# Reordering the opening of a fused attention and two-MLP kernel, and moving batch 1's preparation one step

## The chip, the cores and the metric

One core of one Trainium2 chip runs the whole kernel. The metric is the device time of one execution in microseconds, the median of three runs. The profile is one execution on the same core.

## The reference

All arrays are float32. There are 8 batches of 576 rows and 512 columns (8 heads of 64).

```python
kv = einsum('bhsd,bhse->bhde', k, v)            # 64 x 64 for each head
out = einsum('bhsd,bhde->bhse', q, kv)
out = out / sqrt(mean(out**2, -1) + 1e-6) * g_norm
x = out as (batch, 576, 512)
u = x + real(fft(fft(x, axis=1), axis=2))       # mixing by a 2D transform
un = (u - mean(u)) / sqrt(var(u) + 1e-6)        # over the 512 columns
x2 = u + max(un @ w_ch1, 0) @ w_ch2             # 512 -> 2048 -> 512
u2 = x2 + (x2.T @ U @ V).T                      # rank 32, over the rows
result = u2 + max(u2 @ w2_ch1, 0) @ w2_ch2
```

## The kernel before

**Stages.** The 4608 rows form 9 blocks of 512. A batch is prepared first: the products of keys and values (`kvbd`), the outputs `o` (`t_o`), their norm (`t_norm`), the folds of rows and columns that halve the transform (`t_fold_s`, `t_fold_e`), the high and low parts of the folded columns (`t_fold_h`, `t_fold_l`), the transform over the rows (`t_s1`), and that over the columns (`t_s2`). The first MLP then goes through each block in 16 steps, one for each 128 of the 2048 hidden columns: `emit_l1(n)` makes hidden chunk n by 12 matrix products, `emit_l2(n - 1)` adds the chunk before to four accumulators. The second MLP follows, its last part in groups that don't matter here.

**Order.** The order of instructions is written by hand; each engine takes its own in that order. The opening (`tile_fused_kernel` from line 1220 on) prepares batch 0 whole and normalises and transposes block 0 (`f_stats`, `f_rs`, `f_norm`, `f_tr`), before step 0 starts. `keep_warm(n)` puts n products of the identity, two instructions each, between TensorE's real ones. Batch j + 1 is prepared in the steps of block j: `batch_tasks(b)` gives a list of tasks for each step, and `place` appends them to `side[n]`, which runs at the end of step n. `fill[n]` runs ahead of `emit_l2(n - 1)`. In a step the order is: split of the second weight, `emit_l1(n)`, `w_mags` for the weights that this step converts, `split_w1(n + 2)`, `fill[n]`, `emit_l2(n - 1)`, `side[n]`.

**Weights.** Weights arrive as 64-bit words (the arrays viewed as integers, 512 KB each) and are converted to float32 on the chip: `w_load` (SyncE's queue), `w_mags` (two ScalarE instructions, lines 113 and 114), `conv_a` (VectorE, lines 122 and 123), `conv_b` (VectorE line 128, then the addition of line 130 on VectorE or, for the second of a pair, on GpSimd). Weight 2i is chunk i of the first matrix, 2i + 1 of the second. In step k of block 0 `w_conv` converts weights 6 + 2k and 7 + 2k. `split_w1` takes the high part on ScalarE (line 198) and the low part on GpSimd or VectorE (line 199). There are two `raw` buffers and two `more_raw`; converting a weight frees its buffer, and `w_next` issues the next load.

**Buffers that tie the stages.** `side_bank` gives PSUM banks: in the opening four accumulator banks and two side banks in turn, from step 0 on the two side banks alone. The tables of the transform (`load_table`) land in buffers and are rounded by ScalarE (`round_table`, line 297). The single row 288 has its own tile `e288`, whose high half ScalarE and low half VectorE writes (lines 448 and 461); a product of line 473 reads it. Key and value rows of batches 1 to 4 are loaded early by `kv_load_early`, into buffers of weights that come later.

Batch 1 is one step later than the other batches (`SH = 1`), in these lines:

```python
d = SH if b == 1 else 0
t[c + d][0:0] = [lambda k=k: t_o(b, k) for k in ks]
t[c + d + 4 + p].append(lambda c=c, p=p: t_fold_l(b, c, p))
if d and p:
    fill[9] = lambda: [t_s1(b, 1, e) for e in range(2)]
else:
    t[7 + d + p] += [lambda p=p, e=e: t_s1(b, p, e) for e in range(2)]
```

Of the kernel before, what the change touches and what calls it, by code (L numbers as in the profile page):

```python
# [23 lines left out]
C = 128  # L24
# [21 lines left out]
def kernel(ctx: ExitStack, tc: tile.TileContext, qT, kvm, gn, w1a, w2a, w1b, w2b,  # L46
# [280 lines left out]

    kvt = {}
# [213 lines left out]
    def load_first():  # L542
        kv = at.tile([128, 2, KC, DM], F32, tag="slot_a", name="kv0")
        q = whole(at, [128, 4, NQ], F32, "q0", "slot_c")
        for half in range(2):
            c = slice(256 * half, 256 * half + 256)
            for a in range(2):
                nc.sync.dma_start(out=kv[:, a, :, c], in_=kvm[0][:, a, :, c])
        nc.sync.dma_start(out=q, in_=qT[0])
# [9 lines left out]
    def batch_tasks(b):  # L559

        t = [[] for _ in range(14)]
        d = SH if b == 1 else 0
# [11 lines left out]
        for p in range(2):  # L574
            if d and p:
                fill[9] = lambda: [t_s1(b, 1, e) for e in range(2)]
            else:
                t[7 + d + p] += [lambda p=p, e=e: t_s1(b, p, e) for e in range(2)]
# [49 lines left out]
    def f_new():  # L628
        for w in (6, 2, 1, "b"):
            first[w] = whole(pa, [128, 5, 1 if w == "b" else w], F32, f"first{w}", f"lnf{w}")  # L630
        nc.vector.memset(first[2], 1.0)
# [10 lines left out]
    def f_norm(i):  # L642
# [6 lines left out]
        if i < 3:  # L649
# [570 lines left out]
    with tc.manual_schedule():  # L1220
# [6 lines left out]
        load_table(0)  # L1227
        kv_load_early(1, 6)
        load_table(1)
        load_table(2)  # L1230
        kv_load_early(2, 11)
        for k in range(4):
            w_load(k)
# [7 lines left out]
        keep_warm(15)  # L1241
        t_kv(0, 0)
        t_kv(0, 1)
        for k in range(5):
            t_o(0, k)
        keep_warm(60)
# [6 lines left out]
        round_table(0, 0)  # L1253
# [3 lines left out]
        t_fold_h(0, 1, 0)  # L1257
        t_fold_l(0, 0, 0)
# [3 lines left out]
        t_fold_l(0, 1, 0)  # L1262
        t_fold_l(0, 2, 0)
# [3 lines left out]
        round_table(1, 0)  # L1267
        for c in range(2):
            t_fold_s(0, c, 1)
            t_fold_e(0, c, 1)  # L1270
            if c:
                t_s1_hi(0, 0, 0)
            t_fold_h(0, c, 1)
            if c:
                t_s1_hi(0, 0, 1)
                t_fold_l(0, 0, 1)
            else:
                round_table(2, 0)
        t_fold_s(0, 2, 1)
        t_fold_e(0, 2, 1)  # L1280
        t_fold_h(0, 2, 1)
        t_fold_l(0, 1, 1)
        t_fold_l(0, 2, 1)
        for e in range(2):
            t_s1_lo(0, 0, e)
            round_table(2, 1 + e)
        for e in range(2):
            t_s1(0, 1, e)
        t_s2(0, 2)
# [3 lines left out]
        w_mags(0, 1, 2, 3)  # L1293
# [14 lines left out]
        for i in range(3):  # L1308
            f_norm(i)
        a0 = conv_a(raws.pop(0), w_new(0), pws.pop(0))  # L1310
        for i in (3, 4):
            f_norm(i)
        conv_b(*a0)
        w_next((0,))
# [9 lines left out]
        w_conv(3, 4)  # L1324
# [213 lines left out]
```

## Time and profile before

| | us |
|---|---|
| median of 3 runs (1761.09 to 1761.47) | 1761.33 |
| the profiled execution | 1760.34 |
| its span, first to last instruction | 1758.4 |
| TensorE busy in the span | 1737.7 |
| VectorE busy | 1180.2 |
| ScalarE busy | 832.0 |
| GpSimd busy | 463.8 |

PE is TensorE, DVE VectorE, ACT ScalarE, POOL GpSimd, and L473 is line 473 of the kernel. A float32 product is two instructions, one of the rounded type `fp32r` is one. TensorE's busy time counts the `warm` products too, and its matrix products overlap at their ends, so that the starts in a timeline tell more than the lengths. A row of a timeline gives start, length, engine, line, operation, output and inputs, shape, count, and in brackets the idle time before it and what ended that.

### The profile page before, as it was taken

To read this page: it belongs to the slowest core of one execution; us is meant where nothing else is said; L and a number is where in the kernel's file an instruction comes from. 1 tells how busy PE (TensorE), PEld (TensorE's weight loads), DVE (VectorE), ACT (ScalarE), POOL (GpSimd) and SP (SyncE) were. 2 spreads that over 40 slices of the span, in tenths; PEclk is the share of its full clock that TensorE was granted. 3 is DMA by queue.
4 is the path that set the end of the run, shared out by engine and by line. 5 is a ranking of instruction groups with operands and counts; after the bars stand their busy time and mean duration, and the time that the engine had idled before them with its cause. 6 is when DMAs were issued, how large, how long until landed. Compare 5 with 4: busy or idle time off the path is not lost.

```text
span 1758.4 us, 23273 instructions
## 1 busy us (share of the span) xinstructions
PE 1737.7 (99%) x8246; PEld 1428.3 (81%) x8246; DVE 1180.2 (67%) x1913; ACT 832.0 (47%) x1594; POOL 463.8 (26%) x362
## 2 busy tenths in 40 slices
PE   9999999999999999999999999999999999999999
PEld 9767788888888888888888788878888888888877
DVE  5878777778677686756676667348735963694285
ACT  5674344544334343443555465455345534552253
POOL 2346454554645445442322222000000000000000
PEclk9999999999999999999999999999999999999999
DMA  8755124150613415004378854757776776777675
GB/s 321 239 183 202 49 99 140 37 196 29 222 52 139 156 66 205 25 37 118 111 271 296 315 205 161 243 170 254 244 233 197 242 256 181 224 220 237 190 218 189
DMA packets 130276, 315.25 MB, mean 179 GB/s; under 512 B 20696, under 2 KB 23528, under 8 KB 128368
## 3 DMA queue, kind: packets, MB, share of 16 engines
q1 hardware_dynamic: 130160, 313.77, 53.7%
q8 instruction: 65, 1.06, 0.2%
q14 instruction: 51, 0.42, 0.1%
HBM read 238.83 MB, written 74.88 MB: 178 GB/s over the span
## 4 chain that ended last, share of the span: by engine, by line
PE 93%; DMA 3%; DVE 2%; ACT 1%; issue 1%; SPq 0%; POOL 0%; ACTq 0%; DVEq 0%; POOLq 0%
PE y L1118 10%; PE yy L1198 10%; PE h L223 8%; PE h L225 8%; PE h L224 8%; PE acc L252 7%; PE acc L254 7%; PE acc L253 7%; PE z L1198 5%; PE zz L1118 5%; PE w L1198 3%; PE z L1118 3%; PE o L383 2%; PE pt L814 1%; PE acc L244 1%; PE u L839 1%
## 5 line engine op out<-in xcount | busy, mean ns | idle before, releaser
L199 POOL TENSOR_TENSOR w1l<-w,w1h 128x512 fp32r<-128x512 f32 x147 | 199.2, 1355 | 404.1 <-ACT w1h L198 391.7
L223 PE MATMUL h<-xl,w1h 128*128 128x512 f32 x576 | 232.0, 403 | 2.7 <-DVE xl L668 2.7
L225 PE MATMUL h<-xh,w1l 128*128 128x512 f32 x576 | 226.0, 392 | 0.0
L224 PE MATMUL h<-xh,w1h 128*128 128x512 f32 x576 | 225.5, 392 | 0.0
L252 PE MATMUL acc<-w2h,gl 128*128 128x512 f32 x524 | 205.9, 393 | 0.1
L254 PE MATMUL acc<-w2h,gh 128*128 128x512 f32 x524 | 204.1, 389 | 0.0
L253 PE MATMUL acc<-w2l,gh 128*128 128x512 f32 x524 | 204.0, 389 | 0.0
L232 ACT ACTIVATE gh<-h 128x512 fp32r<-128x512 f32 x147 | 87.7, 596 | 228.4 <-PE h L225 227.9
L1118 PE MATMUL y<-xv,v 128*128 128x512 f32 x768 | 191.8, 394 | 2.7 <-ACT g L1055 2.7
L1055 ACT ACTIVATE g<-y 128x512 f32<-128x512 f32 x128 | 76.7, 599 | 211.5 <-PE y L1118 211.5
L1118 PEld LDWEIGHTS y<-xv,v 128*128 128x128 f32 x768 | 143.6, 187 | 38.4 <-ACT g L1055 4.5
L233 DVE SCALAR_TENSOR_TENSOR gl<-h,gh 128x512 fp32r<-128x512 f32 x147 | 100.7, 685 | 88.3 <-ACT gh L232 88.0
L209 DVE TENSOR_TENSOR w2l<-w,w2h 128x512 fp32r<-128x512 f32 x147 | 136.1, 926 | 26.8 <-ACT w2h L208 26.4
L223 PEld LDWEIGHTS h<-xl,w1h 128*128 128x128 f32 x576 | 109.1, 189 | 24.9 <-issue 4.1
L225 PEld LDWEIGHTS h<-xh,w1l 128*128 128x128 f32 x576 | 108.7, 189 | 24.4 <-POOL w1l L199 0.6
L224 PEld LDWEIGHTS h<-xh,w1h 128*128 128x128 f32 x576 | 109.1, 189 | 22.3 <-issue 1.7
L252 PEld LDWEIGHTS acc<-w2h,gl 128*128 128x128 f32 x524 | 98.3, 188 | 21.8 <-DVE gl L233 2.1
L254 PEld LDWEIGHTS acc<-w2h,gh 128*128 128x128 f32 x524 | 98.4, 188 | 20.6
L253 PEld LDWEIGHTS acc<-w2l,gh 128*128 128x128 f32 x524 | 98.4, 188 | 19.8
L198 ACT ACTIVATE w1h<-w 128x512 fp32r<-128x512 f32 x160 | 99.9, 624 | 25.8 <-DVE w L130 21.5
L208 ACT ACTIVATE w2h<-w 128x512 fp32r<-128x512 f32 x147 | 91.8, 625 | 34.8 <-PE acc L254 31.2
L1049 DVE TENSOR_TENSOR g<-zz,g 128x512 f32<-128x512 f32 x64 | 44.2, 691 | 93.1 <-ACT g L1055 80.1
(237 smaller groups left out, 3675.0 us busy)
## 6 DMA issues: line engine op xcount, KB each, us to landing
v<-wv_d SPq DMA_DIRECT2D x224, 512.0 KB, 3.8
wv_d<-vo SPq DMA_DIRECT2D x112, 256.0 KB, 2.8
kve<-in_kvm SPq DMA_DIRECT2D x40, 256.0 KB, 6.8
q<-in_qT SPq DMA_DIRECT2D x8, 1220.0 KB, 10.5
x_d<-x2o SPq DMA_DIRECT2D x36, 256.0 KB, 2.1
x2f<-x_d SPq DMA_DIRECT2D x36, 256.0 KB, 5.1
outT<-o SPq DMA_DIRECT2D x36, 256.0 KB, 2.4
u_d<-x SPq DMA_DIRECT2D x32, 256.0 KB, 2.6
```

Of the source, the lines that this page charges most:

```text
L198: nc.scalar.activation(out=ah, in_=a, func=AF.Copy)
L199: (nc.vector if n in on_dve else nc.gpsimd).tensor_tensor(out=al, in0=a, in1=f32(ah), op=ALU.subtract)
L209: nc.vector.tensor_tensor(out=cl, in0=c, in1=f32(ch), op=ALU.subtract)
L223: nc.tensor.matmul(out=h, lhsT=ah[:, kc, :], rhs=xl[:, kc, :], start=(kc == 0), stop=False)
L224: nc.tensor.matmul(out=h, lhsT=ah[:, kc, :], rhs=xh[:, kc, :], start=False, stop=False)
L225: nc.tensor.matmul(out=h, lhsT=al[:, kc, :], rhs=xh[:, kc, :], start=False, stop=(kc == 3))
L233: nc.vector.scalar_tensor_tensor(out=gl, in0=h, scalar=0.0, in1=f32(gh), op0=ALU.max, op1=ALU.subtract)
L252: nc.tensor.matmul(out=a, lhsT=gl[:, tt], rhs=ch, start=s, stop=False)
L253: nc.tensor.matmul(out=a, lhsT=gh[:, tt], rhs=cl, start=False, stop=False)
L254: nc.tensor.matmul(out=a, lhsT=gh[:, tt], rhs=ch, start=False, stop=e)
L1118: nc.tensor.matmul(out=dst, lhsT=w[:, c], rhs=r[:, k], start=p in (0, 1, 3) and k + n == 0, stop=k == 1 and n == 2, skip_group_check=True)
L1198: nc.tensor.matmul(out=dst[mp], lhsT=w[:, c], rhs=r, start=p in (0, 1, 6, 3) and i + n == 0, stop=i == 7 and n == 2, skip_group_check=True)
```

## The change

The change touches the opening and steps 0 to 9.

- **Batch 0's loads.** Keys and values come in five row tiles instead of four quarters by columns; q in two pieces. The tables are loaded ahead of batch 1's keys and values, and weight 0 ahead of them too; weights 1 to 3 ahead of batch 2's.
- **Batch 0's products** of keys and values are accumulated tile by tile in one bank (`t_kv_first`), with one copy of each half into `kvbd`. Of the warm products 8 and 52 are left of 15 and 60.
- **Pauses.** The tables are rounded at other places, weight 0's magnitudes are taken and weight 0 is converted ahead of the column transform instead of between the norms of block 0. The folds of the second kind start earlier. The norm of the third part (`f_norm(2)`) moves from ScalarE to VectorE.
- **Small tiles.** `first[1]` and `first["b"]` share one tile.
- **Batch 1.** Outputs, norms and folds start in step 0 (`d = 0`); its row transform stays in step 8 and `fill[9]` (`d1 = SH`).
- **Weights 3 to 7.** `w_conv(4, 3)` takes weight 4 first, so that its addition is VectorE's and weight 3's GpSimd's; the conversion of weight 5 and the magnitudes of 6 and 7 go behind batch 1's tasks in step 0's list.

```diff
@@ -324,6 +324,18 @@
             nc.scalar.activation(out=kvbd[64:128, pairs, 64:128], in_=pv[64:128, :, 64:128], func=AF.Copy)
         else:
             nc.vector.tensor_copy(out=kvbd[64:128, pairs, 64:128], in_=pv[64:128, :, 64:128])
+
+    def t_kv_first():
+        kv = st[0]["kv"]
+        ps = side_bank("kv0")
+        for t in range(KC):
+            for j in range(4):
+                cols = slice(128 * j, 128 * j + 128)
+                nc.tensor.matmul(out=ps[:, cols], lhsT=kv[:, 0, t, cols], rhs=kv[:, 1, t, cols],
+                                 start=(t + j == 0), stop=(t == KC - 1), skip_group_check=True)
+        pv = ps.rearrange("p (j e) -> p j e", j=4)
+        nc.scalar.activation(out=kvbd[0:64, :, 0:64], in_=pv[0:64, :, 0:64], func=AF.Copy)
+        nc.vector.tensor_copy(out=kvbd[64:128, :, 64:128], in_=pv[64:128, :, 64:128])
 
     kvt = {}
 
@@ -542,11 +554,10 @@
     def load_first():
         kv = at.tile([128, 2, KC, DM], F32, tag="slot_a", name="kv0")
         q = whole(at, [128, 4, NQ], F32, "q0", "slot_c")
-        for half in range(2):
-            c = slice(256 * half, 256 * half + 256)
-            for a in range(2):
-                nc.sync.dma_start(out=kv[:, a, :, c], in_=kvm[0][:, a, :, c])
-        nc.sync.dma_start(out=q, in_=qT[0])
+        for t in range(KC):
+            nc.sync.dma_start(out=kv[:, :, t], in_=kvm[0][:, :, t])
+        for c in (slice(0, 2 * C), slice(2 * C, NQ)):
+            nc.sync.dma_start(out=q[:, :, c], in_=qT[0][:, :, c])
         nc.sync.dma_start(out=gnb, in_=gn)
         st[0] = {"kv": kv, "q": q}
 
@@ -559,7 +570,7 @@
     def batch_tasks(b):
 
         t = [[] for _ in range(14)]
-        d = SH if b == 1 else 0
+        d, d1 = 0, SH if b == 1 else 0
         for c in range(3):
             ks = range(2 * c, min(2 * c + 2, 5))
             t[c + d][0:0] = [lambda k=k: t_o(b, k) for k in ks]
@@ -572,10 +583,10 @@
                 t[c + d + 4 + p].append(lambda c=c, p=p: t_fold_l(b, c, p))
             t[c + 9].append(lambda c=c: t_s2(b, c))
         for p in range(2):
-            if d and p:
+            if d1 and p:
                 fill[9] = lambda: [t_s1(b, 1, e) for e in range(2)]
             else:
-                t[7 + d + p] += [lambda p=p, e=e: t_s1(b, p, e) for e in range(2)]
+                t[7 + d1 + p] += [lambda p=p, e=e: t_s1(b, p, e) for e in range(2)]
         if b + 1 < B:
             if b + 1 in EARLY:
                 t[11].insert(0, lambda: kv_back(b + 1))
@@ -626,8 +637,10 @@
         nc.vector.bn_aggr(out=first[2][:m, i], in_=first[6][:m, i])
 
     def f_new():
-        for w in (6, 2, 1, "b"):
-            first[w] = whole(pa, [128, 5, 1 if w == "b" else w], F32, f"first{w}", f"lnf{w}")
+        for w in (6, 2):
+            first[w] = whole(pa, [128, 5, w], F32, f"first{w}", f"lnf{w}")
+        rb = whole(pa, [128, 2, 5, 1], F32, "firstr", "lnfr")
+        first[1], first["b"] = rb[:, 0], rb[:, 1]
         nc.vector.memset(first[2], 1.0)
 
     def f_rs(a, b):
@@ -646,7 +659,7 @@
             z = whole(at, [C, 3, ND], F32, "un_z", "de", 2)
             un[0].insert(0, z.rearrange("p a b -> p (a b)")[:, 0:DM])
         x = st[0]["x"][:m, g, c]
-        if i < 3:
+        if i < 2:
             nc.scalar.activation(out=un[0][i][:m], in_=x, func=AF.Identity, bias=first["b"][:m, i],
                                  scale=first[1][:m, i])
         else:
@@ -1224,13 +1237,13 @@
         nc.vector.memset(f32(e288), 0.0)
         nc.scalar.activation(out=e288, in_=f32(e288), func=AF.Copy)
         load_first()
-        load_table(0)
+        for k in range(3):
+            load_table(k)
+        w_load(0)
         kv_load_early(1, 6)
-        load_table(1)
-        load_table(2)
+        for k in (1, 2, 3):
+            w_load(k)
         kv_load_early(2, 11)
-        for k in range(4):
-            w_load(k)
         done = 6
         f_new()
 
@@ -1238,59 +1251,62 @@
             conv_b(*conv_a(raws.pop(s), w_new(s), pws.pop(s)))
             w_next((s,))
 
-        keep_warm(15)
-        t_kv(0, 0)
-        t_kv(0, 1)
+        keep_warm(8)
+        t_kv_first()
         for k in range(5):
             t_o(0, k)
-        keep_warm(60)
+        keep_warm(52)
+        round_table(0, 0)
         for k in range(3):
             t_norm(0, k)
         t_fold_s(0, 0, 0)
         t_fold_e(0, 0, 0)
         t_fold_h(0, 0, 0)
         t_norm(0, 3)
-        round_table(0, 0)
+        round_table(1, 0)
         t_fold_s(0, 1, 0)
         t_norm(0, 4)
         t_fold_e(0, 1, 0)
         t_fold_h(0, 1, 0)
+        w_mags(0)
         t_fold_l(0, 0, 0)
         t_fold_s(0, 2, 0)
         t_fold_e(0, 2, 0)
         t_fold_h(0, 2, 0)
         t_fold_l(0, 1, 0)
+        round_table(2, 0)
+        t_fold_s(0, 0, 1)
+        t_fold_e(0, 0, 1)
+        t_fold_h(0, 0, 1)
         t_fold_l(0, 2, 0)
         for e in range(2):
             t_s1_mm(0, 0, e)
         t_kve_mm(1, 0)
-        round_table(1, 0)
-        for c in range(2):
-            t_fold_s(0, c, 1)
-            t_fold_e(0, c, 1)
-            if c:
-                t_s1_hi(0, 0, 0)
-            t_fold_h(0, c, 1)
-            if c:
-                t_s1_hi(0, 0, 1)
-                t_fold_l(0, 0, 1)
-            else:
-                round_table(2, 0)
+        t_fold_s(0, 1, 1)
+        t_fold_e(0, 1, 1)
+        for k in range(1, 3):
+            round_table(2, k)
+        t_fold_h(0, 1, 1)
+        t_fold_l(0, 0, 1)
         t_fold_s(0, 2, 1)
         t_fold_e(0, 2, 1)
+        t_s1_hi(0, 0, 0)
         t_fold_h(0, 2, 1)
         t_fold_l(0, 1, 1)
         t_fold_l(0, 2, 1)
+        t_s1_hi(0, 0, 1)
         for e in range(2):
             t_s1_lo(0, 0, e)
-            round_table(2, 1 + e)
+        a0 = conv_a(raws.pop(0), w_new(0), pws.pop(0))
         for e in range(2):
             t_s1(0, 1, e)
+        conv_b(*a0)
+        w_next((0,))
         t_s2(0, 2)
         t_kve_out(1, 0)
         t_s2(0, 0)
         t_s2(0, 1)
-        w_mags(0, 1, 2, 3)
+        w_mags(1, 2, 3)
         load_q(1)
         for i in (1, 2, 0):
             f_stats(i)
@@ -1305,13 +1321,8 @@
         for half in range(2):
             t_kv_early(2, half, "w0_5")
         keep_warm(4)
-        for i in range(3):
+        for i in range(5):
             f_norm(i)
-        a0 = conv_a(raws.pop(0), w_new(0), pws.pop(0))
-        for i in (3, 4):
-            f_norm(i)
-        conv_b(*a0)
-        w_next((0,))
         for i in range(5):
             f_tr(i)
         on_dve.add(0)
@@ -1321,10 +1332,9 @@
         one(1)
         t_u_out(0, 2)
         w_mags(4)
-        w_conv(3, 4)
+        w_conv(4, 3)
         early.clear()
         fill[0] = lambda: [t_kv_early(3, h, "w1_5") for h in range(2)]
-        side[0] += [lambda: w_mags(5), lambda: one(5), lambda: w_mags(6, 7)]
         side[3].append(lambda: kv_load_early(4, 11))
         for n, h in ((6, 0), (7, 1)):
             fill[n] = lambda h=h: t_kv_early(4, h)
@@ -1377,6 +1387,7 @@
         for c in range(4):
             side[NA + 12 + c].append(lambda c=c: v_load(c))
         mags = {}
+        side[0] += [lambda: w_mags(5), lambda: one(5), lambda: w_mags(6, 7)]
         for k, m in enumerate(range(done, 2 * NF, 2)):
             side[k].append(lambda m=m: w_conv(m, m + 1))
             if k:
```

## Rows read from the trace of the kernel before

**Rows 1.** Waits of TensorE after 56 us: total, times, longest.

```profile
PE s L473 <- DVE e L461: 3.9, 1, 3.9
...
PE h L223 <- DVE xl L668: 2.7, 1, 2.7
```

**Rows 2.** Timeline of TensorE before step 0: start, length, idle before.

```profile
10.67 2.47 PE L316 MATMUL kv<-kv 128*128 128x128 f32 x20 [1.25 <-DMA kv<-in_kvm]
13.69 4.68 PE L383 MATMUL o<-kvbd,q 128*128 128x128 f32 x40 [0.55 <-DMA q<-in_qT]
18.21 13.56 PE L399 MATMUL warm<-ident 128*128 128x128 f32 x120
31.53 0.38 PE L469 MATMUL s<-tab,eh 128*128 128x290 f32 x1
...
51.62 2.13 PE L663 MATMUL ftr<-ident,un 128*128 128x128 f32 x16 [0.28 <-ACT un L650]
56.46 0.77 PE L223 MATMUL h<-xl,w1h 128*128 128x512 f32 x1 [2.71 <-DVE xl L668]
```

**Rows 3.** Windows of the opening: engines' busy time, granted clock, DMA share, GB/s.

```profile
7.00:8.00 1.00, 1.00 (x9) 1.00 (x10) 0.00 (x0) 0.00 (x0) 0.00 (x0) 1.00 1.10 349
...
20.00:22.00 2.00, 2.00 (x20) 2.00 (x19) 1.97 (x5) 1.62 (x7) 2.00 (x3) 1.00 1.07 399
```

**Rows 4.** Timeline of VectorE before step 0.

```profile
29.28 0.41 DVE L439 TENSOR_TENSOR ez<-f,ez 32x256 fp32r<-32x256 f32 x1
...
40.04 0.42 DVE L520 TENSOR_TENSOR de<-s,de 34x258 f32<-34x258 f32 x1 [1.04 <-ACT de L519]
...
51.53 1.00 DVE L653 TENSOR_SCALAR un<-x,first,first 128x512 f32<-128x512 f32 x2
...
53.16 0.69 DVE L130 CUSTOM_DVE_ANT_0 w<-w,cv 128x1024 uint16<-128x1024 uint16 x1
53.77 2.54 DVE L668 TENSOR_TENSOR xl<-ftr,xh 128x132 fp32r<-128x132 f32 x5
```

**Rows 5.** Groups of VectorE's instructions by line, 0 to 56 us.

```profile
L424 DVE TENSOR_TENSOR f<-x 128x512 f32<-128x512 f32 (+1 forms) x6 | 4.1, 685 | 0.4 <-ACT x L412 0.2
...
L429 DVE TENSOR_TENSOR f<-f 128x256 f32<-128x256 f32 (+1 forms) x6 | 2.5, 421 | 0.2
```

**Rows 6.** Windows of 4 us around step 8.

```profile
128.00:132.00 4.00, 3.59 (x12) 3.28 (x13) 3.86 (x9) 2.29 (x5) 0.00 (x0) 0.50 0.16 40
132.00:136.00 4.00, 4.00 (x15) 3.21 (x15) 3.31 (x7) 3.08 (x8) 2.72 (x2) 0.70 0.80 256
```

**Rows 7.** Timeline of TensorE, steps 1 and 8.

```profile
65.01 0.48 PE L223 MATMUL h<-xl,w1h 128*128 128x512 f32 x1
...
71.26 1.95 PE L383 MATMUL o<-kvbd,q 128*128 128x128 f32 x16
...
128.41 0.61 PE L473 MATMUL s<-tab,e 97*128 97x290 f32 x1 [3.87 <-DVE e L461]
```

**Rows 8.** Timeline of ScalarE, step 0.

```profile
67.42 0.63 ACT L198 ACTIVATE w1h<-w 128x512 fp32r<-128x512 f32 x1 [4.16 <-POOL w L130]
67.95 1.13 ACT L363 ACTIVATE kvr<-kve 64x128 f32<-64x128 f32 x4
```

**Rows 9.** Timeline of VectorE, steps 0 and 6 to 9.

```profile
64.72 0.69 DVE L130 CUSTOM_DVE_ANT_0 w<-w,cv 128x1024 uint16<-128x1024 uint16 x1
...
97.77 1.39 DVE L429 TENSOR_TENSOR f<-f 128x256 f32<-128x256 f32 x1
...
127.17 0.43 DVE L458 TENSOR_TENSOR eh<-f,eh 128x256 fp32r<-128x256 f32 x1 [2.87 <-ACT eh L445]
...
127.94 0.42 DVE L461 TENSOR_TENSOR e<-f,e 1x256 fp32r<-1x256 f32 x1
...
139.78 0.82 DVE L502 TENSOR_TENSOR y<-s,y 128x290 fp32r<-128x290 f32 x2
```

**Rows 10.** Timeline of GpSimd, step 4.

```profile
97.21 1.66 POOL L130 TENSOR_TENSOR w<-w,cv 128x512 uint32<-128x512 uint32 x1 [1.77 <-PE h L225]
```

## The prediction

> **What bounds the kernel now.** I read the table of waits first, then the timeline of each engine, stage by stage. The waits of TensorE from 56 us to the end name only two gaps longer than 1 us: 2.7 us before the first matrix product of step 0 (line 223, waiting for `xl` of line 668) and 3.9 us in step 8 (line 473, waiting for the low half of `e288`, line 461) [rows 1]. From step 9 on TensorE is fed, and the change leaves its work there as it is. So the time can only move in two stretches: the opening up to 56.46 us, and steps 0 to 9.
>
> In the opening TensorE is not the limit. Between 18.21 and 31.53 us it runs 120 `warm` products, which compute nothing that is kept [rows 2]. The reader should follow VectorE instead: low half of `ez` at 29.28, `de` at 40.04, `un` at 51.53, weight 0's last addition at 53.16 and the five `xl` from 53.77 to 56.31 [rows 4]; step 0 starts 0.15 later.
>
> In steps 0 to 8 VectorE and ScalarE run about a step behind TensorE. At 124.3 VectorE idles for 2.87 us for ScalarE, and then makes `e288`'s low half at 127.94, for which TensorE has stood since 124.54 [rows 7, 9]. Behind that gap the granted clock is 0.50 for 3.59 us of work, then 0.70 over the next 4 us [rows 6]: 1.8 + 1.2 = 3.0 us lost at the lower of the two levels (1.2 against 2.4 GHz). Step 8 thus costs 3.87 + 3.0 = 6.9 us.
>
> All sums are against the profiled execution, 1760.34 us (span 1758.4 and 1.94 around it), 0.99 below the median of 1761.33. A change within 0.2%, 3.5 us, I count as none.
>
> **The change part by part.**
>
> *A. Key and value of batch 0 by row tiles, q in two pieces.* Before, the second half of key and value lets TensorE start at 10.67; its ten products take 2.47, the copies into `kvbd` the 0.55 to 13.69, where the outputs start; q lands at about the same time [rows 2]. After, the products of four row tiles lie under the transfer of the next, and a fifth of 4.94 us, 0.99, remains after the last byte. The copies are twice as wide: between 0.55 and 1.1, I take 0.85, since both are short instructions with a fixed part. The runs in memory grow from 1 to 2 KB. While the 1 KB runs moved the DMA made 349 GB/s; where 2 KB runs and tables moved, 399 [rows 3]. For 2.62 MB that is 7.5 against 6.6 us, so arrival at about 9.7 instead of 10.6. Outputs can start at 9.7 + 0.1 + 0.99 + 0.85 = 11.6. The first 0.52 MB of q need 1.5 us more at 349 GB/s (11.2), the rest 2.1 (13.3); it is due when two of five output tiles are done, 11.6 + 1.9 = 13.5. I take **-1.9 us**. Without a better rate it is -1.0; with all copies at 0.55, -2.3.
> The Trainium skill, "DMA: Bandwidth & Descriptors", section "Why small descriptors are slow", names a fixed cost of about 3 beats beside 32-byte beats; as an estimate, 1 KB to 2 KB then gives 4% (0.3 us, not 0.9), and A would be -1.3. The rows above show 14%, on a mix of shapes.
>
> *B. Tables rounded in other pauses, weight 0 converted there, folds reordered, 52 instead of 60 and 8 instead of 15 warm products.* Sixteen instructions of 0.113 go, 1.8 us [rows 2]. But the low half of `ez`, which the first transform needs, now stands behind one more pair of folds (0.69 + 0.42 [rows 5]): it is ready at 29.69 + 1.1 = 30.8 instead of 29.69, and the transform starts there, 0.8 before 31.53. Of weight 0's four conversion instructions two now stand ahead of `y`'s second pair and two ahead of `de`, where VectorE waits 1.04 us; two as long as the last one, 0.69, overrun that by 0.35 [rows 4], which the lighter ScalarE queue (its table roundings lie earlier) should return. I take **-0.8**, between +0.4 (neither) and -1.8 (all of the warm products). What hides the moved roundings and weight 0's two magnitudes is ScalarE's waiting for norms and folds; if that cover is gone, the folds are late next, and rival 2 prices it. Fewer bytes for small tiles and the shared tile for `first[1]` and `first["b"]` I cost at nothing: writers and readers keep their order on their engines.
>
> *C. Nothing of weight 0 between the norms and `xl`.* Before, the additions end at 53.85 and five `xl` of 0.51 follow [rows 4]. After, VectorE has one norm more (0.50) and no conversion. Norms end at 52.53; five `xl` then end at 55.07 at the earliest, and the last transposition, which ends at 53.75 [rows 2], leaves 1.3 us for one copy and one subtraction. **-1.25**, between -0.5 (if the high halves on ScalarE are late) and -1.7.
>
> *D. Batch 1's outputs and folds a step earlier, its transform still in step 8.* `e288`'s low half is then made in step 6's list, a step earlier. From 65.01, where step 1 begins, to the gap at 124.54 lie eight steps [rows 7], 7.4 us each, against a wait of 3.87. **-6.9**. If the granted clock falls elsewhere in its place, -3.9.
>
> *E. The price in step 0.* Batch 1's first two output tiles now come right behind batch 3's key-value products, which filled both side banks. TensorE is free for them at 65.01 [rows 7]. The banks empty by two ScalarE copies each (1.13 for four), queued behind the high half of weight 4, which now waited for GpSimd until 67.42 [rows 8]. With the order 4, 3 VectorE finishes weight 4 itself, at 64.72 + 0.69 = 65.41 [rows 9]; then 0.63 and 0.57 make 66.6. TensorE waits 66.6 - 65.0 = **+1.6**, between 0 and 2.7 (if ScalarE is also held up by g). The queue behind it is step 1; VectorE's next, `x`, waits too, but weight 6 has the time of the two tiles (1.95 [rows 7]) more. Moving weight 5 to 7 behind the two tiles costs nothing for the same reason.
>
> *F. VectorE in step 9.* Its run from 127.17 to the end of `y`'s low half at 140.60 has work throughout [rows 6, 9], and TensorE, at the lower clock for a part of it, came no earlier than its end. After, TensorE arrives 6.9 - 1.6 = 5.3 us earlier against the start of step 0, 78.8 us after it instead of 84.1. VectorE ended weights 18 and 19 at 124.30, 67.8 us after it; the wait of 2.87 goes and four folds of about 0.4 move ahead, so that 13.4 - 1.6 = 11.8 remain: 79.6, or 0.8 late. GpSimd can add to it (rival 1): I take **+1.2**, between 0 and 3.5.
>
> Sum: -1.9 - 0.8 - 1.25 - 6.9 + 1.6 + 1.2 = -8.0 us. 1760.34 - 8.0 = 1752.3 for a profiled execution, 1761.33 - 8.0 = **1753.3** for the median.
>
> **The rivals.**
>
> *1. The wait of step 8 comes back as others.* VectorE's fold of 256 columns took 1.39 us where one without company took 0.42 (mean of six), since GpSimd's addition ran from 97.21 to 98.87 [rows 5, 9, 10]. If the folds a step earlier meet as many of these, the weights' low halves come late in steps 7 to 9 and F is at its end and half as much again, +5. For it: the chain is dense at both ends. Against: VectorE still idled 2.87 us at once as late as in step 7 [rows 9]. Time: -8.0 + 3.8 = -4.2, 1757.1.
>
> *2. The opening gains nothing but C*, because the DMA rate stays and ScalarE's queue, with the moved roundings, holds the folds: A -1.0, B +0.8. Time: -8.0 + 0.9 + 1.6 = -5.5, 1755.8. Rows 3 speak against it, the fold order for it.
>
> *3. Slower.* Each of steps 3 to 8 has up to three long GpSimd instructions (lines 130, 199, 424), and one that meets VectorE costs it 1.39 - 0.42 = 1.0 us. If two more of the three meet it in each step, VectorE falls 2.0 us a step behind, and once its lead is used up the weights' low halves make TensorE wait: up to 12 us in six steps in place of F's 1.2, so -8.0 - 1.2 + 12 = +2.8: 1764.1. It decides from 9.2 / 6 = 1.5 us a step on. Against: the trace of before has the same three in its steps, and TensorE stood only in step 8 [rows 1].
> The Trainium skill, "SBUF — State Buffer", section "Who interferes with whom", says that VectorE's and GpSimd's shared port pair is an exclusive lock and that the loser blocks fully; the 1.39 us agree with it, and by that rule rivals 1 and 3 are the ways in which this change fails.
>
> *4. More than forecast:* no wait in step 0 or 9: -10.8, 1750.5.
>
> **How the numbers follow.** Forecast 0.58; rival 1 0.15; rival 2 0.15; rival 3 0.05; rival 4 0.07. The forecast's own bounds (A 0.9, B 1.2, C 0.7, E and F 1.5 each way, independent, some 2.6 together) give 1750.7 to 1755.9. To leave out no more than 2 in 10 the range takes in rivals 1 and 2: 1750.3 to 1757.8, which leaves out rival 3, half of rival 4 and the tails of 1. Faster by over 0.2% (below 1757.8): the forecast and rival 4, 0.65, with 0.13 of rival 2 and 0.09 of rival 1, which lies only 0.7 below, less 0.02 of tails: 0.85; slower 0.05; within 0.2% the other 0.10.
>
> **What would show it.** A: the first output product at about 11.6 to 11.9. B: first transform about 2.7 earlier than 31.53, `de` likewise. C: `xl` right behind the norms; step 0's first product near 52.5. D: no gap at line 473, no lower clock in step 8. E: a gap of 1 to 2 us before batch 1's first outputs in step 0. F: small gaps at line 469 or 515 in steps 9 and 10. It is wrong if gaps of more than 2 us stand in steps 3 to 9, if the products of step 0 start after 54.5, or if the granted clock falls to its lower level behind step 0's gap.

## The result, and the profile after

The changed kernel takes 1745.81 us (median of four runs, 1744.85 to 1746.37), against 1761.4 for the kernel before beside it: a ratio of 0.9908, 95% interval 0.9891 to 0.9926, 15.6 us less. The forecast was 1753.3, with a range from 1750.3 to 1757.8. The sign was right; the gain is twice the forecast, and hardly any of it lies where the prediction looked for it.

The groups named below are the last part of the second MLP. The description of the kernel before says that they don't matter here; nearly the whole gain lies in them. There are four groups, each of two halves with 56 units. A unit is six products of 512 columns that read one part of a buffer of `v`. Each product has two operands in the chip's memory: the stationary tile (`v`), which a weight load of its own (PEld in the trace) takes in, and the moving tile of 512 columns. In the first half the moving tile is one of seven, three of them `x0` to `x2`; in the second half it is a split weight or g.

Lines of `kernel.py` stand 12 or 13 further down after the change: 383 is 395, 469 is 481, 668 is 681, 1118 is 1131, 1198 is 1211.

The start of each stage in the two traces (us) tells where the time went:

| first product of | before | after | difference |
|---|---|---|---|
| step 0 | 56.46 | 59.51 | +3.05 |
| step 8 | 116.85 | 121.52 | +4.67 |
| step 10 | 142.23 | 143.32 | +1.09 |
| the groups of the second MLP | 1097.15 | 1096.70 | -0.45 |
| end of the last product | 1754.67 | 1739.16 | -15.51 |

The opening became 3.05 longer (forecast -3.95). Steps 0 to 9 became 1.96 shorter (forecast -4.1). The groups, where no instruction was touched, became 15.06 shorter: 657.5 before, 642.5 after. The stretch between became 1.54 shorter (954.92 to 953.38).

The opening of the changed kernel, timeline of TensorE (start, length, idle before and its releaser), to be held against [rows 2]:

```profile
9.74 2.44 PE L334 MATMUL kv<-kv 128*128 128x128 f32 x16 [0.18 <-DMA kv<-in_kvm]
13.11 0.49 PE L395 MATMUL o<-kvbd,q 128*128 128x128 f32 x2 [0.93 <-DVE kvbd L338]
16.82 7.22 PE L395 MATMUL o<-kvbd,q 128*128 128x128 f32 x38 [3.22 <-DMA q<-in_qT]
23.88 11.78 PE L411 MATMUL warm<-ident 128*128 128x128 f32 x104
35.41 0.38 PE L481 MATMUL s<-tab,eh 128*128 128x290 f32 x1
...
59.51 0.47 PE L223 MATMUL h<-xl,w1h 128*128 128x512 f32 x1 [1.96 <-DVE xl L681]
```

Behind the last row tiles one output product (two instructions) runs, and the other 19 (38 instructions) wait 3.22 us for q. Why it was late is in SP's timeline of the transfers (start, length, number):

```profile
4.09 8.80 SPq L560 DMA_DIRECT2D q<-in_qT  x2
12.93 0.62 SPq L561 DMA_DIRECT2D gnb<-in_gn  x1
13.59 1.87 SPq L284 DMA_DIRECT2D tab_in<-in_tab  x4
```

and in the table of what its queue waited for:

```profile
SPq L560 <- DMA q<-in_qT: 7.6, 1, 7.6
```

The second piece of q was issued 7.6 us late, once the first had landed, and the tables, the weights and batch 1's rows stand behind it in the same queue. The windows of 1 us (TensorE's busy time, granted clock, DMA share, GB/s) show that little or nothing is transferred from 11 to 14 us:

```profile
10.00:11.00 1.00, 0.90 (x8) 1.00 0.95 339
11.00:12.00 1.00, 0.97 (x8) 1.00 0.20 69
12.00:13.00 1.00, 0.18 (x2) 1.00 0.00 0
13.00:14.00 1.00, 0.49 (x2) 1.00 0.39 50
```

Behind the wait the granted clock is at 0.50, the lower of its two levels, from 16 to 22 us, so that the 38 instructions take 7.22 us.

TensorE's waits from 56 us on (total, times, longest), to be held against [rows 1]:

```profile
PE h L223 <- DVE xl L681: 2.0, 1, 2.0
PE s L481 <- DVE y L514: 1.9, 1, 1.9
...
PE o L395 <- ACT kvr L375: 1.0, 1, 1.0
PE s L527 <- DVE y L514: 1.0, 1, 1.0
```

The wait of 3.9 in step 8 is gone. Others have come: 1.0 in step 0 before batch 1's outputs (line 395) and 1.9 + 1.0 in step 9 (lines 481 and 527).

The groups: windows of 20 us near the end with the products of lines 1198 and 1211 alone, first of the kernel before, then of the changed one (TensorE's busy time and number of products, granted clock, DMA share, GB/s):

```profile
1700.00:1720.00 20.00, 20.00 (x88) 1.00 0.78 241
```

```profile
1700.00:1720.00 20.00, 20.00 (x90) 1.00 0.72 227
```

TensorE is busy all the time at the full granted clock (2.4 GHz) in both, and yet 90 products go where 88 went. From start to start, a 512-column product of the groups takes 233.0 ns in the median before and 227.0 after. Summed over the groups' 2631 pairs of neighbours of one line that is 617.8 against 603.0 us, 14.8 less, which is nearly the whole gain. In the first MLP (from 150 to 880 us) both kernels have 227. The groups' table by form shows it as a longer record, before and after:

```profile
L1118 PE MATMUL y<-xv,v 128*128 128x512 f32 x768 | 191.8, 394 | 2.7 <-ACT g L1055 2.7
L1118 PE MATMUL zz<-xv,v 128*128 128x512 f32 x384 | 98.6, 392 | 0.0
```

```profile
L1131 PE MATMUL y<-xv,v 128*128 128x512 f32 x768 | 187.4, 390 | 2.7 <-ACT g L1068 2.7
L1131 PE MATMUL zz<-xv,v 128*128 128x512 f32 x384 | 97.4, 389 | 0.0
```

What could lengthen the same instruction at the same clock? The small tiles of the first norms took 320 bytes a partition and now take 256. All that is allocated behind them moved down by 64 bytes: `v` and `x0` to `x2` of the groups lay 64 bytes past a multiple of 256 and now lie at one. The tiles ahead of them (`xh`, `xl`, `un`, `res`, the split weights, g) lie at multiples in both. So before, `v` lay unlike most of the moving tiles, and now all lie alike. The moving tiles of the hidden products in the second MLP's first block, which stand ahead of the groups, lie behind the small tiles too: these products take 227.5 ns now and 229.8 before, a part of the 1.54 us.

### The profile page after: what moved, and what is told of

The parts are those of the page before. It is cut to its first block, busy times and chain, and to the rows that moved or that the text cites. A ratio compares the mean times of both kernels' runs of the same rounds, so it can differ in the third digit from the quotient of the medians.

```text
span 1743.1 us, 23211 instructions
## 1 busy us (share of the span) xinstructions
PE 1719.5 (99%) x8216; PEld 1427.3 (82%) x8216; DVE 1180.7 (68%) x1913; ACT 830.2 (48%) x1592; POOL 462.8 (27%) x362
## 4 chain that ended last, share of the span: by engine, by line
PE 87%; DVE 1%; POOL 1%; DMA 1%; ACT 1%; issue 0%; SPq 0%; DVEq 0%; ACTq 0%; POOLq 0%
PE y L1131 10%; PE yy L1211 10%; PE h L223 7%; PE h L224 7%; PE h L225 7%; PE acc L252 6%; PE acc L254 6%; PE acc L253 6%; PE z L1211 5%; PE zz L1131 5%; PE z L1131 2%; PE w L1211 2%; PE o L395 2%; PE pt L827 1%; PE u L852 1%; PE kv L316 1%
## 5 line engine op out<-in xcount | busy, mean ns | idle before, releaser
L223 PE MATMUL h<-xl,w1h 128*128 128x512 f32 x576 | 231.5, 402 | 2.0 <-DVE xl L681 2.0
L1131 PE MATMUL y<-xv,v 128*128 128x512 f32 x768 | 187.4, 390 | 2.7 <-ACT g L1068 2.7
```

The costliest lines, as they stand in the source:

```text
L223: nc.tensor.matmul(out=h, lhsT=ah[:, kc, :], rhs=xl[:, kc, :], start=(kc == 0), stop=False)
L1131: nc.tensor.matmul(out=dst, lhsT=w[:, c], rhs=r[:, k], start=p in (0, 1, 3) and k + n == 0, stop=k == 1 and n == 2, skip_group_check=True)
```

## Experiments

The kernel before, run beside each set of experiments, took 1760.4 to 1761.6. Ratios are to it.

### Is it the place of the tiles or the order of the work?

The first kernel is the one before with its small tiles merged as in the change; the second is the changed one without that; the third has 128 more bytes:

```diff
-        for w in (6, 2, 1, "b"):
-            first[w] = whole(pa, [128, 5, 1 if w == "b" else w], F32, ...)      # 320 bytes
+        for w in (6, 2):
+            first[w] = whole(pa, [128, 5, w], F32, ...)
+        rb = whole(pa, [128, 2, 5, 1], F32, "firstr", "lnfr")                   # 256; third: [128, 48], 384
```

> The kernel before with one part of the change alone: its four small tiles take 256 bytes a partition where they took 320, so that all that is allocated behind them lies 64 bytes lower (the groups' stationary tiles v at a multiple of 256 bytes, where before they lay 64 bytes past one). Order, queues and the first steps stay as before. Place theory (the 64 bytes shorten the products of the second MLP's groups): the pitch of the 512-column products there falls from 233 to 227 ns, some 2630 of them give 15 us, and the median is 1746, with step 10 of the first MLP starting where it did before. Order theory (the new order of the opening and of the first steps gives the time): pitch 233 ns, and 1761.

> The changed kernel with the small tiles in 320 bytes a partition again, and so all that lies behind them 64 bytes past a multiple of 256; every other part of the change stays. Place theory: the groups' pitch is 233 ns again and the median 1761 to 1763 (the later start of step 10, +1.1, stays). Order theory: 1746.

> The changed kernel with 128 bytes more behind its small tiles, so that the tiles behind them lie 128 bytes past a multiple of 256. Place theory, if whole 256 bytes count: the groups' pitch is 233 ns and the median about 1761. Place theory, if 128 bytes are enough: 227 ns and 1746. Order theory: 1746.

Measured: 1743.77 (0.9902, 0.9887 to 0.9917) for the tiles alone, 1761.83 (1.0007, 0.9997 to 1.0016) for all but the tiles, 1760.07 (0.9995, 0.9985 to 1.0005) with 384 bytes. The groups took 642.5, 657.5 and 655.6 us. The tiles alone give 17.3 us, as much as the whole change; everything else together gave nothing that can be measured. The order theory falls. The third kernel shares its tile as the change does, so the sharing is not what helps. A displacement by 128 bytes costs nearly as much as one by 64 (13.2 us in the groups, against 15.1). The window near the end, as above, for the tiles alone, and one of the same length for all but the tiles:

```profile
1700.00:1720.00 20.00, 20.00 (x90) 1.00 0.71 221
```

```profile
1715.00:1735.00 20.00, 20.00 (x88) 1.00 0.69 212
```

### Which tiles, and how far displaced?

A helper around the groups' pool leaves bytes free ahead of chosen tiles:

```diff
-            pb = pbx["pb"] = ctx.enter_context(tc.tile_pool(name="pb", bufs=1))
+            pb = pbx["pb"] = Shifted(ctx.enter_context(tc.tile_pool(name="pb", bufs=1)), PADS)
+ # v: the five buffers of v at 0, 32, 64, 128, 192    x: {"x0": 64, "vs": 192, "x1": 128, "x2": 128}
+ # pool back (on the kernel with 320 bytes): {"o": 192}
```

> The version with the query block in one transfer (1741.1, all tiles at multiples of 256 bytes), with the five buffers of the stationary tile v placed by hand 0, 32, 64, 128 and 192 bytes past a multiple of 256 and the moving tiles left where they are. Stationary theory (what counts is where the weights of a product lie): the pitch follows the buffer that is read, 227 ns for the one at 0 and 230 to 235 for the others, and the median is about 1741 + 0.8 x 15 = 1753. Moving theory (only the place of the moving tiles counts): 227 ns for all five, 1741. Traffic theory (the loads that write into a displaced buffer disturb the products that run meanwhile): the pitch rises in the stretch in which a displaced buffer is written, one buffer before it is read, and does not follow the buffer read.

> The same version with the stationary tiles v at a multiple of 256 bytes and two of the seven moving operands of the groups' first half displaced: the tile x0 (operand 3 of 7) by 64 bytes, x1 (operand 6) by 128. Stationary theory: 227 ns for all products, 1741. Moving theory: 16 of the 56 units in each first half run slower, by 6 ns or so on 96 products a group and four groups, 2 us at most: 1743, and the pitch tells it, 227 for the other five operands and 230 or more for these two.

> The changed kernel with the small tiles in 320 bytes (which took 1761.8), and 192 bytes left free ahead of the pool that holds v and x0 to x2 (and the outputs' and the last norms' tiles), so that this pool alone is back at multiples of 256; the weights, the groups' G tiles, the attention's tiles and the raw weights stay 64 bytes past one. If the products' operands are all that counts: pitch 227 ns in the groups and 1746, as the changed kernel. If VectorE's and ScalarE's access to the displaced G tiles, or the loads into displaced weights, carry a part: between 1746 and 1762 by that part.

Measured: 1750.63, 1746.42 (one run each) and 1747.00 (0.9916, 0.9901 to 0.9931). With the pool of `v` and `x0` to `x2` back and everything else still displaced, the products of the groups are at 227 and the groups take 643.0 us: the products' operands are enough, and the displaced G tiles, weights and their loads carry no part that can be seen.

In the kernel with five places of `v` the moving tiles lie at multiples of 256, and each buffer of `v` serves two units in a row. Mean start to start (ns) of the first five products of a unit, second halves of the groups:

| `v` read lies past a multiple of 256 by | 0 | 32 | 64 | 128 | 192 bytes |
|---|---|---|---|---|---|
| first unit of a buffer | 229.2 | 232.4 | 233.8 | 233.4 | 229.2 |
| second unit | 227.2 | 233.4 | 233.6 | 232.7 | 229.0 |

The pitch, as this time from start to start is called here, follows the buffer that is read, and the groups take 654.3 us, 11.8 more than 642.5, where 12 were expected. What stands beside counts as well: the last product of the second unit at 0, behind which the weights of the buffer at 32 come, takes 234.7, and the first unit at 0, which follows the buffer at 192, 229.2. So the traffic theory falls. But the moving theory, as the other side had it, falls only by half: in the kernel with displaced `x0` and `x1` and `v` at 0, the operands 3 and 6 run at 231.7 and 232.0, and the second half of the groups at 227.1. Either operand can do it. The groups take 646.4 us, 4.0 longer where 2 at most were expected, since units behind a displaced one are longer as well: 231.5 for operand 5, which lies at a multiple of 256 and follows operand 3. (The rest of the 5.3 by which this kernel is slower lies ahead of the groups.)

### Must both operands lie at a multiple of 256, or only alike?

Two kernels on the version with q in two contiguous ranges (below), one with an unused tile of 64 bytes ahead of everything, one with it ahead of the split weights alone:

```diff
     muT = whole(com, [128, NT // 128], F32, "muT")
+    off = com.tile([128, 16], F32, name="off")            # all displaced by 64
     wsp = ctx.enter_context(tc.tile_pool(name="wsp", bufs=2))
+    wsp.tile([128, 16], F32, name="off", bufs=1)          # or: the split weights alone,
     gpool = ctx.enter_context(tc.tile_pool(name="gpool", bufs=2))
+    gpool.tile([128, 48], F32, name="on", bufs=1)         # the rest at multiples of 256
```

> The version with the query block in two contiguous ranges (1740.0), with one unused tile of 64 bytes ahead of all that is placed behind it: both operands of every 512-column product, of the first MLP too, now start 64 bytes past a multiple of 256. Nothing else changes. Place theory: some 6370 products (1920 of the hidden layers, 1764 of the output layers, 2688 in the groups) run longer by 3.3 ns (as those of before whose two operands were both displaced, 230 ns) to 6.6 ns (as those with one displaced, 233), 21 to 42 us together: 1761 to 1782. If the effect belongs to the groups alone: 1755. If the two displacements cancel when both are the same: 1740.

> The version with the query block in two contiguous ranges (1740.0), with the split weights w1 and w2 of the MLPs (and they alone) 64 bytes past a multiple of 256 and all other tiles at multiples. One operand of each hidden product (1920) and of each output product of the split steps (1764) is then displaced against the other, and of two thirds of the groups' second half (some 900). Difference theory (a product is longer when its two operands lie differently within 256 bytes): these 4580 run at 233 instead of 226.7 ns, 29 us together, and the median is 1765 to 1770, with the pitch of the first MLP at 233. Groups theory (the effect needs something of the groups, as their loads): pitch 227 in the first MLP and 1740 to 1746.

Measured: 1739.96 (0.9878, 0.9863 to 0.9893) with everything displaced, and 1760.34 (0.9997, 0.9987 to 1.0006) with the weights alone. The first was a surprise: it costs nothing, and the groups' products run at 226.8 ns in the first halves and 227.0 in the second. I had expected 1761 to 1782. So it is not the multiple of 256 that counts but the difference of the two operands' places within 256 bytes. The second kernel shows the same in the first MLP, where both kernels of the change had none: hidden products 233.3 ns, output products 231.2 (227.8 and 227.2 without the displacement). It costs 20.3 us in all, 15.7 of them between step 10 and the groups; 25 to 30 were expected, as the output products, whose moving tile is the displaced one, lose less. A stretch of 50 us of this kernel (products of all kinds, granted clock, DMA share, GB/s):

```profile
600.00:650.00 50.00, 50.00 (x242) 1.00 0.06 22
```

In it the transfers move 22 GB/s, and the products are at 233.4 and 231.1 ns all the same: no traffic is needed for it.

The kernel before fits only in part: the units of `x0` to `x2`, where both operands lay 64 bytes past a multiple, ran at 229.9 ns, and all others at 233.3. They stand among unlike ones.

### Why was the opening longer?

First q in one transfer, then q's two pieces in two contiguous ranges of their tile:

```diff
-        for c in (slice(0, 2 * C), slice(2 * C, NQ)):
-            nc.sync.dma_start(out=q[:, :, c], in_=qT[0][:, :, c])
+        nc.sync.dma_start(out=q, in_=qT[0])                                  # whole
+        q = [q[:, 8 * C * i:8 * C * i + 4 * w].rearrange("p (j n) -> p j n", j=4)
+             for i, w in enumerate((2 * C, NQ - 2 * C))]                     # apart
+        for v, c in zip(q, (slice(0, 2 * C), slice(2 * C, NQ))):
+            nc.sync.dma_start(out=v, in_=qT[0][:, :, c])
```

> The changed kernel with the query block of batch 0 in one transfer behind the five row tiles, where the change has two. If the two pieces are what delays the opening (the 38 products waited 3.22 us for the second piece, until 16.82), the wait shrinks by about 3, the first MLP product comes at 56.5 instead of 59.51, and the median is about 1743. If the five row tiles or the tables behind them cost the time, q lands as late as now and the median stays at 1746.

> The changed kernel with the two pieces of the query block in two contiguous ranges of their tile, where the change has interleaved ones (rows of 256 and 354 columns inside rows of 610). If the second piece's transfer stands in SP's queue until the first has landed because the two ranges of one tile are taken to overlap (it was issued at 12.35, after 7.6 us of waiting, with all tables behind it), the wait goes, no transfer pauses at 11 to 13.5 us, the second piece lands by 14 and the first MLP product starts at 55 to 56: 1740 to 1742. If another cause holds it (the count of transfers in flight), it is issued at about 12 again: 1746.

Measured: 1741.13 (0.9888, 0.9873 to 0.9902) and 1740.01 (0.9879, 0.9863 to 0.9896), 4.7 and 5.8 below the changed kernel. TensorE's timeline with the pieces apart:

```profile
9.69 2.43 PE L334 MATMUL kv<-kv 128*128 128x128 f32 x16 [0.20 <-DMA kv<-in_kvm]
13.04 4.71 PE L396 MATMUL o<-kvbd,q 128*128 128x128 f32 x40 [0.93 <-DVE kvbd L338]
```

and SP's:

```profile
4.15 1.41 SPq L562 DMA_DIRECT2D q<-in_qT  x2
...
10.93 0.33 SPq L102 DMA_DIRECT2D raw<-in_w1a  x1
```

Both pieces are issued within 1.41 us, no transfer pauses, and step 0 starts at 53.32. The 40 instructions of the outputs take 4.71 us at the full granted clock. So the wait stood between two transfers into interleaved column ranges of one tile, 256 of 610 columns and the other 354 in each of four rows; the count of transfers in flight was not the cause.

### What are the other parts worth without that wait?

The rows by tiles and q apart without the rest of the opening, on the kernel before with 256 bytes; then, on the version with q apart, weight 0's conversion between the norms again (and the third norm on ScalarE), and batch 1's outputs, norms and folds a step later again:

```diff
+        t_kv_first()                                      # rows alone: with load_first as above
-        a0 = conv_a(raws.pop(0), w_new(0), pws.pop(0))    # conversion back: from behind t_s1_lo
+        a0 = conv_a(raws.pop(0), w_new(0), pws.pop(0))    #   to behind f_norm(2)
-        d, d1 = 0, SH if b == 1 else 0
+        d = d1 = SH if b == 1 else 0                      # outputs late
```

> The kernel before with the small tiles in 256 bytes (1743.77), and of the new opening only the key and value rows by tiles and the query block in two contiguous pieces; the tables, the conversion of weight 0 and batch 1 stay as before. Prediction's first term (-1.9): the first x on VectorE comes 1.9 earlier than at 15.5, the first MLP starts at 54.6 instead of 56.49, and the median is 1741.9. If the opening behind the first outputs is bound by VectorE's and ScalarE's own order and not by its start: 56.5 and 1743.8.

> The version with the query block in two contiguous ranges (1740.0), with the conversion of weight 0 between the first norms again, as in the kernel before (and ScalarE doing three of the five norms). Prediction's third term (1.25): the first MLP starts at 54.6 instead of 53.32 and the median is 1741.2. If moving the conversion only shifted VectorE's work, because it is VectorE that sets the opening in both places: 53.3 and 1740.

> The version with the query block in two contiguous ranges (1740.0), with batch 1's outputs, norms and folds a step later again, as in the kernel before. By the sum of the prediction for this part (-6.9 + 1.6 + 1.2 = -4.1) it takes 1744.1, and step 8 of the first MLP holds the wait for the sequence tables' products again (14.4 us long instead of 8.7). By the steps of the two traces (steps 0 to 9 take 2.4 us less with the part than without) 1742.4. If the place of the tiles was all, and this part nothing: 1740.0.

Measured: 1744.16 (0.9904, 0.9887 to 0.9920), 1740.59 (0.9882, 0.9868 to 0.9897) and 1739.15 (0.9877, 0.9862 to 0.9892). By the starts of step 0, the rows alone give 0.58 (56.49 to 55.91), the conversion 0.79 (54.11 to 53.32); medians can't tell such sizes. The early outputs and folds give nothing: 1739.15 without them, 1740.01 with them. With them late, this one wait stands in step 8:

```profile
123.58 0.44 PE L486 MATMUL s<-tab,e 97*128 97x290 f32 x1 [2.68 <-DVE e L474]
```

It is 2.68 and no longer 3.87: VectorE makes this half 69.5 us after the start of step 0, and 71.5 before. Steps 0 to 9 take 83.43 us so, and 83.36 with early outputs: step 8 is 4.33 shorter, step 9 2.07 longer, and steps 0 to 3 together 2.5 longer. Of these, 1.03 are the wait for `kvr`; most of the rest is the clock. Windows of the first products of step 0, early outputs first, then late:

```profile
54.00:57.00 3.00, 3.00 (x9) 0.53 0.93 316
```

```profile
54.00:57.00 3.00, 3.00 (x17) 1.00 0.99 338
```

Up to here both programs are the same and waited the same 1.95 us for `xl`; the granted clock fell in one and not in the other, where it fell in step 8 instead, behind the 2.68 us. Of the sixteen kernels here without the warming products below, thirteen have the fall around the start of step 0. So a part of this comparison is chance. The last three kernels ask what remains: the outputs late and only the folds early, warming products in that wait, and both.

```diff
-            t[c + d][0:0] = [lambda k=k: t_o(b, k) for k in ks]
-            t[c + d + 1] += [lambda k=k: t_norm(b, k) for k in ks]
+            t[c + d1][0:0] = [lambda k=k: t_o(b, k) for k in ks]
+            t[c + d1 + 1] += [lambda k=k: t_norm(b, k) for k in ks]
         for i in range(5):
             f_tr(i)
+        keep_warm(14)                                     # warming; both: all of it
```

> The version with the query block in two contiguous ranges (1740.0), with batch 1's outputs and norms a step later again and only its folds early. If the price of the change's early outputs is the wait of TensorE in step 0 (1.03, for the copy kvr on ScalarE) and its gain lies in the folds, this takes 1739, with no wait before the outputs and none for e in step 8. If the folds can't be made earlier without the norms (VectorE is as late in step 8 as with all of it late, 2.7 of waiting), 1739 to 1740 with that wait back.

> The version with the query block in two contiguous ranges, with 14 products of no use behind the five transposes, where TensorE waits 1.95 for xl; there its granted clock fell to 0.5 at 54.2 for some 3 us in step 0 (and didn't in the run with late outputs, whose program is the same up to there). If that idle time is what lets the clock fall, it stays at 1.0, step 0 takes 10.4 instead of 12.0, and the median is 1738.4. If the clock falls anyway, 1740; if the products delay the first hidden product, up to 1741.

> The two edits of the last two kernels together, outputs late with folds early, and 14 warming products behind the transposes. If both work: 1737.4; if only the warming does, 1738.4; if neither, 1740.

Measured: 1740.33 (0.9884, 0.9867 to 0.9900), 1738.53 (0.9873, 0.9859 to 0.9888) and 1739.21 (0.9881, 0.9866 to 0.9895). With the folds alone early the wait before the outputs goes, and one for the low half of a weight comes in step 6:

```profile
PE s L482 <- DVE y L515: 1.6, 1, 1.6
PE h L225 <- POOL w1l L199: 1.5, 1, 1.5
PE s L528 <- DVE y L515: 0.9, 1, 0.9
```

With the warming the clock holds at 1.00 through step 0, which takes 11.0 instead of 12.0, but step 0 starts at 54.40 instead of 53.32, and step 10 at 136.98 instead of 136.68: nothing is gained by there. The median that was expected came by luck: the trace is ahead of q apart only between step 10 and the groups (953.3 against 955.1 us), where q apart waits 1.9 us in all for split weights that the edit doesn't touch, and the warmed kernel 0.4. These three, the late outputs and q apart can't be told from one another; all five are 5 to 7 us below the changed kernel and 20 to 22 below the one before, and beat both.

## Why the prediction was off

**The step that failed.** "Fewer bytes for small tiles and the shared tile for `first[1]` and `first["b"]` I cost at nothing: writers and readers keep their order on their engines." This one edit gives all of the gain, 17.3 us alone. The argument looked at who waits for whom, and no wait explains the gain; it didn't ask what else the bytes move. That the sign came out right is luck: without this edit the change gains nothing (1.0007). With it falls "From step 9 on TensorE is fed, and the change leaves its work there as it is": TensorE was fed and its work the same, but a product of the groups was in the median 6 ns longer than its like in the first MLP. The trace of before showed that (233 against 227 from start to start; by the length of the record 394 against 389 to 393 on five of its six lines), and I never compared the two. Shown by the tiles alone, all but the tiles, the pool back, the five places and the two displaced versions; why the difference within 256 bytes lengthens a product was not tried, and stays open.

**A, rows by tiles and q in two pieces (-1.9).** It cost 3.65 (first `x` on VectorE at 19.14 instead of 15.49), by a wait of SP that I never named, though both pieces go into one tile on one queue, and by the lower clock behind it. Without that wait the term is -0.6 (14.87): outputs start at 13.04, not 11.6. (From 13.69 to 11.6 is -2.1, of which the prediction took -1.9.) The copies take 0.93, close to the 0.85 forecast, but the rows come no earlier. With the pieces apart, the transfer of weight 0 is held until the fifth row tile has landed, and is issued at 10.93; before, the second half let TensorE start at 10.67 [rows 2]. The better rate for longer runs shows (401 GB/s from 7 to 9 us in the changed kernel, 349 and 351 before), but not the 0.9 us in the arrival: from 2 to 6 us the rate is lower, 294 against 323.
The estimate by the Trainium skill, "DMA: Bandwidth & Descriptors", section "Why small descriptors are slow", was 0.3 us; the arrival doesn't show that either.

**B and C (-0.8, -1.25).** With q apart, first `x` to step 0 takes 38.45 us against 40.97: -2.5 for the two, forecast -2.05. The sum is right; of its parts, the conversion alone gives 0.79 (forecast 1.25), which leaves 1.7 for B (forecast 0.8). In the changed kernel only -0.6 is left, since its tables, behind q in SP's queue, come late.

**D, E and F (-6.9, +1.6, +1.2).** Each mechanism showed: the low half of `e288` 63.9 us after the start of step 0 instead of 71.5, no wait and full clock in step 8, a wait of 1.0 before the outputs in step 0, waits of 1.9 and 1.0 in step 9. The sizes made the sum: step 8 gave 4.3 to 5.7, step 9 took 2.1, the first steps 2.5 with the clock. By its outcome that is rival 1, the wait that comes back as others, down to nothing instead of half. Of the cause that rival 1 names, folds of VectorE that meet GpSimd's additions, the traces show a little: six folds of 256 columns over 0.8 us in steps 0 to 8 of the changed kernel, four before.

**The sum.** Without the wait for q, the change's order of work starts step 10 5.55 us earlier than before (136.68 against 142.23), where -8.0 was forecast; with it, 1.09 later. The forecast's -8 is not what the measured -15.6 consists of.

## To carry to other kernels

When a tile's size changes, list what moves behind it, and compare the start-to-start time of the same product in all stages of the trace: a stage that is 3% slower at full clock and without a gap is a finding. Here it paid to place the two operands of all products alike within 256 bytes; where that needs padding, it costs some bytes. When a transfer is cut in two, look in the queue's own timeline whether the second piece waits for the first; contiguous ranges of the tile did not.

## What was not expected of the hardware

- Where all products have their stationary and their moving tile alike within 256 bytes, all at 0 or all at 64, a product of 512 columns takes 227 ns from start to start. It takes about 233 when the stationary tile lies 32, 64 or 128 bytes past the moving one, and 229 to 232 at 192. Weight loads show nothing of it: 187 ns a record before, 188 after. Why the places matter stays open.
- The products beside such ones are longer too: the units of the kernel before whose own operands lay alike ran at 229.9 ns.
- The granted clock fell to 0.5 behind a wait of 1.95 us in one program and not in another that is the same up to there. A prediction can't have such a fall, or its absence, for certain.
